# Attention by 32 states and a squared-ReLU MLP on one core: tiny tiles in a pool of their own, another token order for x, clamps of the weight decode on VectorE, program order held on TensorE, a new order of steps

## The chip, the cores and the metric

The kernel runs on one core of a Trainium2 chip. Its engines, as the profile names them, are PE (TensorE, matrix products; PEld is its weight load), DVE (VectorE), ACT (ScalarE), POOL (GpSimd) and SP (SyncE, which here issues nearly all DMAs). Each engine takes its instructions in the order of its own queue, and an instruction waits there for the semaphores of what it needs. The metric is device time in microseconds (us) of one execution; lower is better.

## The reference

```python
# x: 8 batches x 8 heads x 512 tokens x 64, state: 8 x 8 x 32 x 64, w_in: 512 x 2048, w_out: 2048 x 512
scores = scale * x @ state^T;   a  = softmax(scores, last axis);   xread = a  @ state
scores2 = scale * state @ x^T;  a2 = softmax(scores2, last axis);  sread = a2 @ x
y = concatenate([xread, sread], axis=2)          # per batch 512 + 32 rows, heads side by side: 512 columns
h = maximum(y @ w_in, 0);  out = (h * h) @ w_out # 4352 rows
```

The weights come as 64-bit floats, the rest as 32-bit floats, and the output is 32-bit.

## The kernel before, in words

**Products in three parts.** A 32-bit value is split into a high part that TensorE takes in its fast fp32r format and the low rest. Each product is then three matmuls: high by high, high by low, low by high (`mm3`, line 284). `split` (line 265) makes the parts: ACT rounds the high part, DVE or POOL subtracts it.

**The weights are decoded on the chip.** `load_raw` (line 500) and `load_wo` (604) bring 512 KB pieces of the 64-bit weights, 16 of each. `decode` (297) turns one piece into 32-bit floats: ACT takes the absolute value of the high words (line 303), a clamp follows (304, on DVE or on POOL), and three DVE instructions shift and join the bits (305 to 307). `decode_wi` decodes half of a column block of `w_in` (256 columns, `hb` = 0 to 7) and stores it to DRAM for later; `prep_wo` decodes a row block of `w_out` (`fc` = 0 to 15) and splits it into parts that stay in SBUF.

**Attention.** The scores of a batch have only 32 states per head, so state @ w_in is computed once for each pair of batches and column block (`direct_w2`, `later_w2`, `last_w2`; the products are "w2"). The first product of the MLP for tokens is then softmax(scores) times w2, with 256 rows to contract. The batches 0 to 5 keep w2 in DRAM and load it back (`load_w2`), 6 and 7 store it already split. For each batch: `start` and `load` issue the loads of x, `prep` brings x into transposed form (batches 0 and 1 by TensorE, `px`; the others by DVE's 32 by 32 stream transpose, line 364), `scores` multiplies by the states, `transposed_scores`, `softmax` and `exp_s` make the two softmaxes, `transposes` and `sread` the reads for the states. x for batches 2 to 7 comes in 16 DMAs a batch (line 352), each for 32 partitions, in runs of 32 floats.

**The MLP.** `hidden(blk, fc)` (617) makes one block of 128 hidden rows for the 512 tokens of batch `blk`: 6 matmuls into `ph` (two PSUM buffers), ReLU and square on ACT or on ACT and DVE, and the split into `g_hi` (ACT) and `g_lo` (DVE, line 641). `accumulate(blk, fc)` (644) adds its product with `w_out`: 12 matmuls into `acc`. Block 8 holds the 256 rows of the states and has 12 narrower matmuls per hidden step and 6 per accumulate.

**What sets the order.** `PLAN` (line 24) is the program order of all steps, written by hand; `accumulate` runs two to three steps behind `hidden`. The framework then schedules the instructions of each engine by a model of their times, with the program order as priority, so that an engine's queue can differ from `PLAN` unless `keep_in_program_order` ties an instruction behind the one traced before it on its engine. Before the change that is done for the loads of `w_out` and for runs of small matmuls (`in_a_row`, 311). Batches 0 and 1 alternate in groups of four `fc` (0.0 to 0.3, 1.0 to 1.3, 0.4 ...), because the decode of the weights goes on beside them. `SECOND` (183) lists, per kind of operation, the cases that take the second of two engines: for `decode_wi` and `decode_wo` the second is POOL, for `w_out_lo`, `sm_sub`, `sm_mul`, `k_lo`, `w2_lo` it is DVE, for `xT`, `eT`, `out`, `w2_out` it is DVE instead of ACT. The small per-row results of the softmaxes (`m1`, `s1`, `m2`, `nb2`, `s2`, `r2`) lie in the same pool, `p2`, as the large tiles.

Of the kernel before, what the change touches and what calls it, by code (L numbers as in the profile page):

```python
# [19 lines left out]
F64_HI_MIN = 2.0**-15  # L20
# [17 lines left out]
    hidden.0.5 decode_wi.9 load_raw.11 direct_w2.4 prep_wo.8 accumulate.1.3
    hidden.0.6 decode_wi.10 decode_wi.11 load_raw.12 load_wo.10 states.2 accumulate.0.4
    hidden.0.7 load_raw.13 direct_w2.5 load_wo.11 decode_wi.12 accumulate.0.5  # L40
    hidden.1.4 prep_wo.9 load_raw.14 accumulate.0.6
    hidden.1.5 decode_wi.13 load_wo.12 load_raw.15 direct_w2.6 prep_wo.10 load_w2.0.4 load_wo.13
        accumulate.0.7
    hidden.1.6 decode_wi.14 decode_wi.15 direct_w2.7 load_wf.1.0 start.2 load.2.1 prep_wo.11 accumulate.1.4
# [3 lines left out]
    hidden.0.10 later_w2.2.2 later_w2.2.4 load_wf.1.3 prep_wo.14 load_w2.0.7 accumulate.0.8
    hidden.0.11 prep.2.1 prep_wo.15 accumulate.0.9
    hidden.0.12 scores.2 transposed_scores.2.0 exp_s.2.0 transposed_scores.2.1 exp_s.2.1 load_w2.1.4  # L50
        accumulate.0.10
# [155 lines left out]
def tile_attn_moe(  # L207
# [56 lines left out]

    def split(hi, lo, src, key):

        nc.scalar.copy(hi, src)  # L267
        pick(key, nc.gpsimd, nc.vector).tensor_sub(lo, src, hi.bitcast(F32))  # L268
# [42 lines left out]
    def in_a_row(calls):  # L311

        for i, call in enumerate(calls):
            if i == 0:
                call()  # L315
                continue
# [556 lines left out]
```

## Time and profile before

| what | value |
|---|---|
| runs | 740.28, 741.85, 741.93 us; median 741.85 |
| the profiled execution | 738.05 us, span 736.3 us |
| mean granted TensorE clock | 0.988 |
| instructions | 11411 |
| PE, PEld busy | 681.8 and 516.6 us |
| DVE, ACT, POOL busy | 388.5, 335.1 and 130.6 us |
| DMA | 100.36 MB, mean 136 GB/s |

The span runs from the first to the last instruction. A row of a table of windows gives, for a stretch of the span, the busy time of each engine with the number of its instructions, then the granted clock of TensorE (1.00 is full speed), the mean busy share of the 16 DMA engines and what they moved. In a timeline row the columns are start, duration, engine, line, operation, output<-input, shape, count, and in brackets how long the engine had been idle and what it waited for.

### The profile page before, as it was taken

How to read it: one execution, taken by the hardware profiler on the slowest of the kernel's cores; microseconds unless marked ns; L12 is line 12 of the kernel's file. 1: busy time of each engine (PE TensorE's matmuls, PEld its weight loads, DVE VectorE, ACT ScalarE, POOL GpSimd, SP SyncE). 2: the span in 40 equal slices, each digit the busy share in tenths (PEclk: the TensorE clock that was granted, in tenths of full speed). 3: DMA queues.
4: the chain of work that ended last, by engine and by line, in shares of the span. 5: the costliest groups of instructions: out<-in, count | busy, mean ns of one | idle time of the engine just before them, and what ended most of it. 6: DMA issues, size and time to landing. Idle time of an engine off the chain costs nothing.

```text
span 736.3 us, 11411 instructions
## 1 busy us (share of the span) xinstructions
PE 681.8 (93%) x4365; PEld 516.6 (70%) x4365; DVE 388.5 (53%) x665; ACT 335.1 (46%) x643; POOL 130.6 (18%) x92
## 2 busy tenths in 40 slices
...
GB/s 233 280 155 147 100 231 220 190 260 302 59 237 213 188 256 195 72 72 145 163 42 109 146 170 75 69 148 139 58 86 144 60 83 78 94 57 58 29 1 85
DMA packets 120711, 100.36 MB, mean 136 GB/s; under 512 B 68049, under 2 KB 96977, under 8 KB 120657
## 3 DMA queue, kind: packets, MB, share of 16 engines
...
q14 instruction: 21, 0.16, 0.1%
q10 hardware_dynamic: 144, 0.13, 0.1%
...
## 4 chain that ended last, share of the span: by engine, by line
PE 74%; DVE 7%; issue 6%; DMA 5%; SPq 3%; ACT 2%; POOL 2%; DVEq 0%; ACTq 0%; POOLq 0%
PE acc L290 45%; PE ph L290 23%; PE w2ps L318 2%; DMA wi_raw<-in_moe_w_in_dram 2%; SPq L352 1%; DMA wo_raw<-in_moe_w_out_dram 1%; PE w2ps L315 1%; POOL dec L304 1%; DVE dec L307 1%; PE pr L318 1%; DVE wf L306 1%; DMA std<-in_state_dram 1%; DVE dec L306 1%; PE st L315 1%; DMA xp<-in_x_dram 1%
## 5 line engine op out<-in xcount | busy, mean ns | idle before, releaser
L290 PE MATMUL acc<-wo,g_hi 128*128 128x512 f32 x1086 | 322.5, 400 | 0.3 <-ACT g_hi L636 0.3
L290 PEld LDWEIGHTS acc<-wo,g_hi 128*128 128x128 f32 x1086 | 204.0, 189 | 54.8 <-issue 3.5
L290 PE MATMUL ph<-k_hi,w 128*128 128x512 f32 x512 | 185.6, 404 | 6.4 <-DVE g_lo L641 3.9
L290 PE MATMUL acc<-wo,g_lo 128*128 128x512 f32 x543 | 191.4, 397 | 0.0
L641 DVE TENSOR_TENSOR g_lo<-ph,g_hi 128x512 fp32r<-128x512 f32 (+1 forms) x140 | 92.1, 658 | 145.2 <-ACT g_hi L636 141.1
L290 PEld LDWEIGHTS ph<-k_hi,w 128*128 128x128 f32 x512 | 97.3, 191 | 41.5 <-DVE g_lo L641 9.5
L290 PEld LDWEIGHTS acc<-wo,g_lo 128*128 128x128 f32 x543 | 101.0, 189 | 24.9 <-issue 2.1
L636 ACT CAST g_hi<-ph 128x512 fp32r<-128x512 f32 (+1 forms) x144 | 81.1, 564 | 63.3 <-DVE ph L635 57.8
L290 PE MATMUL ph<-k_lo,w 128*128 128x512 f32 x256 | 102.2, 399 | 0.0
L635 DVE SCALAR_TENSOR_TENSOR ph<-ph,r 128x512 f32<-128x512 f32 (+1 forms) x76 | 50.1, 659 | 93.3 <-ACT r L634 93.3
L634 ACT ACTIVATE r<-ph 128x512 f32<-128x512 f32 (+1 forms) x76 | 43.3, 570 | 108.4 <-PE ph L290 108.3
L630 ACT ACTIVATE ph<-ph 128x512 f32<-128x512 f32 (+1 forms) x68 | 38.8, 570 | 76.7 <-PE ph L290 76.7
L268 POOL TENSOR_TENSOR w<-w_f,w 128x512 fp32r<-128x512 f32 x19 | 24.8, 1304 | 216.2 <-ACT w L267 190.0
L290 PEld LDWEIGHTS ph<-k_lo,w 128*128 128x128 f32 x256 | 48.7, 190 | 12.2 <-issue 1.6
L631 ACT ACTIVATE ph<-ph 128x512 f32<-128x512 f32 (+1 forms) x68 | 38.8, 570 | 1.4
L318 PE MATMUL w2ps<-wf,sT 64*32 64x256 f32 x960 | 37.7, 407 | 0.9 <-ACT w L554 0.5
L268 POOL TENSOR_TENSOR s<-sf,s 128x512 fp32r<-128x512 f32 x8 | 10.4, 1299 | 138.2 <-ACT s L267 138.2
L315 PE MATMUL w2ps<-wf,sT 64*32 64x256 f32 x64 | 21.0, 409 | 13.9 <-DVE r L409 7.8
L304 POOL TENSOR_SCALAR wf<-wf 128x512 f32<-128x512 f32 x13 | 26.3, 2027 | 39.1 <-ACT wf L303 35.6
L304 POOL TENSOR_SCALAR dec<-dec 128x512 f32<-128x512 f32 x13 | 26.8, 2070 | 30.9 <-ACT dec L303 30.9
L364 DVE STREAM_TRANSPOSE xT<-xp 128x512 f32<-128x512 f32 x24 | 25.0, 1089 | 13.7 <-DMA xp<-in_x_dram 11.5
L267 ACT CAST w<-w_f 128x512 fp32r<-128x512 f32 x40 | 24.6, 614 | 3.8 <-DMA w_f<-w_d 3.7
...
## 6 DMA issues: line engine op xcount, KB each, us to landing
...
```

The costliest lines, as they stand in the source:

```text
L268: pick(key, nc.gpsimd, nc.vector).tensor_sub(lo, src, hi.bitcast(F32))
L290: m = nc.tensor.matmul(ps, l, r, start=first and i == 0, stop=last and i == len(seq) - 1, skip_group_check=skip)
L304: eng.tensor_scalar(vf, vf, F64_HI_MIN, F64_HI_MAX, ALU.max, ALU.min)
L315: call()
L318: tc.keep_in_program_order(call())
L364: nc.vector.transpose(xT[:, c].rearrange("p (k s j) -> p k j s", k=KC, j=4), self.xp[g][:, c].rearrange("p (j k d) -> p k j d", j=4, k=KC),)
L630: nc.scalar.activation(ph, ph, AF.Relu)
L631: nc.scalar.activation(ph, ph, AF.Square)
L634: nc.scalar.activation(r, ph, AF.Relu)
L635: nc.vector.scalar_tensor_tensor(ph, ph, 0.0, r, ALU.max, ALU.mult)
L636: nc.scalar.copy(ghi, ph)
L641: nc.vector.tensor_sub(glo, ph, ghi.bitcast(F32))
```

## The change

Six edits:

1. The six tiny tiles go from pool `p2` to a new pool `p3` of the same depth.
2. The DMAs of x for batches 2 to 7 write the tokens in the order (k, j) instead of (j, k) along a partition, so that the stream transpose reads and writes 512 elements in one run each; before, both sides were strided.
3. Of 26 clamps on POOL, 24 go to DVE: all 13 of `decode_wo` and 11 of 13 of `decode_wi` (6 and 10 stay).
4. `behind` ties ten chosen DVE instructions to the DVE instruction traced before them: the clamps of `decode_wi` 2, 7, 15 and `decode_wo` 0, 1, 2, 12, and the first reduction of `exp_s` 0.0, 0.1, 2.1.
5. From step `hidden.2.8` on, every TensorE instruction is held in program order.
6. `PLAN` is rewritten up to `hidden.2.4`, and a few entries of `SECOND` change engine (`k_lo.1.0`, `w2_lo.1.5`, `w_out_lo.10`, `xT.1.1.1` to DVE; `k_lo.2.1` to POOL; `w2_out.2.2.1` to ACT; `hidden.1.12` squares on DVE instead of ACT).

```diff
-    load_raw.0 load_states.0 ident neg_ident load_raw.1 start.0 load.0.1 decode_wi.0 load_wo.1 decode_wi.1
-        states.0 prep.0.0 prep.0.1 load_raw.2 scores.0 start.1 load.1.1 direct_w2.0 transposed_scores.0.0
-        exp_s.0.0 softmax.0.0 load_raw.3 load_wo.0 transposed_scores.0.1 exp_s.0.1 softmax.0.1 decode_wi.2
-        decode_wi.3 prep_wo.0 direct_w2.1 prep.1.0 load_wo.2 prep.1.1
-    hidden.0.0 prep_wo.1 load_wo.3 transposes.0
-    hidden.0.1 scores.1 transposed_scores.1.0 exp_s.1.0 transposed_scores.1.1 exp_s.1.1 prep_wo.2 load_raw.4
-    hidden.0.2 load_raw.5 softmax.1.0 softmax.1.1 load_wo.4 sread.0 accumulate.0.0
-    hidden.0.3 decode_wi.4 decode_wi.5 load_wo.5 load_raw.6 load_raw.7 accumulate.0.1
-    hidden.1.0 direct_w2.2 transposes.1 prep_wo.4 load_wo.6 load_wo.7 accumulate.0.2
-    hidden.1.1 decode_wi.6 decode_wi.7 prep_wo.3 sread.1 load_raw.8 load_raw.9 accumulate.0.3
+    load_raw.0 ident neg_ident start.0 load.0.1 load_states.0 load_raw.1 states.0 decode_wi.0 prep.0.0
+        load_raw.2 load_wo.0 decode_wi.1 direct_w2.0 prep_wo.0 load_wo.1 decode_wi.2 start.1 load.1.1
+    prep_wo.1 load_raw.3 decode_wi.3 prep.0.1 scores.0 transposed_scores.0.1 softmax.0.1 exp_s.0.1
+        transposed_scores.0.0 softmax.0.0 exp_s.0.0 hidden.0.0 load_wo.2 load_wo.3
+    hidden.0.1 prep_wo.2 prep.1.0 prep.1.1 scores.1 transposed_scores.1.0 load_raw.5 transposed_scores.1.1
+        load_raw.4
+    prep_wo.3 softmax.1.0 softmax.1.1 load_wo.4 accumulate.0.0
+    exp_s.1.0 exp_s.1.1 direct_w2.1 hidden.0.2 hidden.0.3 transposes.0 sread.0 load_wo.5 accumulate.0.1
+    hidden.1.0 decode_wi.4 load_raw.6 decode_wi.5 load_raw.7 direct_w2.2 load_wo.6 load_wo.7 accumulate.0.2
+    hidden.1.1 transposes.1 prep_wo.4 decode_wi.6 load_raw.8 decode_wi.7 direct_w2.3 load_raw.9
+        accumulate.0.3
...
-    hidden.1.12 load_part.1 accumulate.1.10
-    hidden.1.13 load_w2.2.0 later_w2.6.2 later_w2.6.4 load_wf.1.7 accumulate.1.11
-    hidden.1.14 start.3 accumulate.1.12
-    hidden.1.15 load_wf.2.0 load_w2.2.1 later_w2.7.2 load.3.1 later_w2.7.4 accumulate.1.13
+    hidden.1.12 start.3 load_part.1 accumulate.1.10
+    hidden.1.13 load_wf.1.7 accumulate.1.11 load_w2.2.0
+    hidden.1.14 accumulate.1.12
+    hidden.1.15 load_w2.2.1 later_w2.7.2 later_w2.7.4 load_wf.2.0 accumulate.1.13
     hidden.2.0 accumulate.1.14
     hidden.2.1 load_w2.2.2 accumulate.1.15
-    hidden.2.2 prep.3.0 accumulate.2.0
-    hidden.2.3 load_w2.2.3 accumulate.2.1
-    hidden.2.4 last_w2.0 load_wf.2.1 accumulate.2.2
+    hidden.2.2 load.3.1 prep.3.0 accumulate.2.0
+    hidden.2.3 later_w2.6.2 load_w2.2.3 accumulate.2.1
+    hidden.2.4 later_w2.6.4 last_w2.0 load_wf.2.1 accumulate.2.2
     hidden.2.5 prep.3.1 load_w2.2.4 accumulate.2.3
...
+PINNED_FROM = "hidden.2.8"
...
-    decode_wi: 1 4 5 6 7 8 9 10 11 12 13 14 15
-    decode_wo: 0 1 2 3 4 6 7 8 9 11 13 14 15
+    decode_wi: 6 10
...
+    pin: decode_wi.2 decode_wi.7 decode_wi.15 decode_wo.0 decode_wo.1 decode_wo.2 decode_wo.12 exp_s.0.0
+        exp_s.0.1 exp_s.2.1
...
+    p3 = ctx.enter_context(tc.tile_pool(name="p3", bufs=2))
...
+    def behind(key, op):
+
+        if f"pin.{key}" in second:
+            tc.keep_in_program_order(op)
...
-        nc.tensor.matmul(ps, neg["ident"], hi, start=False, stop=True, skip_group_check=True)
+        in_order(nc.tensor.matmul(ps, neg["ident"], hi, start=False, stop=True, skip_group_check=True))
+
+    pinned = []
+
+    def in_order(m):
+
+        if pinned:
+            tc.keep_in_program_order(m)
+        return m
...
-            if pin:
+            if pin or pinned:
                 tc.keep_in_program_order(m)
...
-        eng.tensor_scalar(vf, vf, F64_HI_MIN, F64_HI_MAX, ALU.max, ALU.min)
-        nc.vector.tensor_scalar(v, v, 3, 0x3FFFFFFF, ALU.logical_shift_left, ALU.bitwise_and)
+        clamp = eng.tensor_scalar(vf, vf, F64_HI_MIN, F64_HI_MAX, ALU.max, ALU.min)
+        if eng is nc.vector:
+            behind(key, clamp)
+        shift = nc.vector.tensor_scalar(v, v, 3, 0x3FFFFFFF, ALU.logical_shift_left, ALU.bitwise_and)
+        if eng is nc.gpsimd:
+            behind(key, shift)
...
             if i == 0:
-                call()
+                in_order(call())
                 continue
...
+                        x_v = x[b, 4 * g + 2 * c + h].rearrange("(j s k) d -> s k j d", j=4, k=KC)
                         nc.sync.dma_start(
-                            xp[o : o + 32, c].rearrange("p (t d) -> p t d", d=32),
-                            x[b, 4 * g + 2 * c + h].rearrange("(s t) d -> s t d", s=32)[..., 32 * e : 32 * e + 32],
+                            xp[o : o + 32, c].rearrange("p (k j d) -> p k j d", k=KC, d=32),
+                            x_v[..., 32 * e : 32 * e + 32],
                         )
...
-                    nc.vector.transpose(
-                        xT[:, c].rearrange("p (k s j) -> p k j s", k=KC, j=4),
-                        self.xp[g][:, c].rearrange("p (j k d) -> p k j d", j=4, k=KC),
-                    )
+                    nc.vector.transpose(xT[:, c], self.xp[g][:, c])
...
-            nc.vector.transpose(sp, self.st[g])
+            behind(f"transposed_scores.{b}.{g}", nc.vector.transpose(sp, self.st[g]))
...
-            m2 = p2.tile([P, 1], F32, tag="m2", name=f"m2{b}_{g}")
-            nc.vector.tensor_reduce(m2, st, AX.X, ALU.max)
+            m2 = p3.tile([P, 1], F32, tag="m2", name=f"m2{b}_{g}")
+            behind(f"exp_s.{b}.{g}", nc.vector.tensor_reduce(m2, st, AX.X, ALU.max))
...
-                    nc.tensor.transpose(pt[:, ts(k, P)], e2[:, k], ident)
+                    in_order(nc.tensor.transpose(pt[:, ts(k, P)], e2[:, k], ident))
...
+        if k == PINNED_FROM:
+            pinned.append(k)
```

More of the change, by code (lines that the diff above doesn't have):

```diff
@@ L31 @@
-    hidden.0.2 load_raw.5 softmax.1.0 softmax.1.1 load_wo.4 sread.0 accumulate.0.0
-    hidden.0.3 decode_wi.4 decode_wi.5 load_wo.5 load_raw.6 load_raw.7 accumulate.0.1
-    hidden.1.0 direct_w2.2 transposes.1 prep_wo.4 load_wo.6 load_wo.7 accumulate.0.2
-    hidden.1.1 decode_wi.6 decode_wi.7 prep_wo.3 sread.1 load_raw.8 load_raw.9 accumulate.0.3
-    hidden.1.2 direct_w2.3 prep_wo.5 prep_wo.6 accumulate.1.0
-    hidden.1.3 prep_wo.7 load_wo.8 load_wo.9 accumulate.1.1
-    hidden.0.4 load_states.2 decode_wi.8 load_raw.10 accumulate.1.2
@@ L38 @@
[L38 to L44, printed above, removed]
@@ L45 @@
-    hidden.1.7 load_w2.0.5 later_w2.0.2 later_w2.0.4 load_wf.1.1 prep_wo.12 load_wo.14 accumulate.1.5
-    hidden.0.8 load_wo.15 later_w2.1.2 later_w2.1.4 load_wf.1.2 prep_wo.13 load_w2.0.6 accumulate.1.6
+    load_raw.0 ident neg_ident start.0 load.0.1 load_states.0 load_raw.1 states.0 decode_wi.0 prep.0.0
+        load_raw.2 load_wo.0 decode_wi.1 direct_w2.0 prep_wo.0 load_wo.1 decode_wi.2 start.1 load.1.1
+    prep_wo.1 load_raw.3 decode_wi.3 prep.0.1 scores.0 transposed_scores.0.1 softmax.0.1 exp_s.0.1
+        transposed_scores.0.0 softmax.0.0 exp_s.0.0 hidden.0.0 load_wo.2 load_wo.3
@@ new lines @@
+    hidden.1.2 prep_wo.5 sread.1 accumulate.1.0
+    hidden.1.3 prep_wo.6 prep_wo.7 load_wo.8 load_wo.9 accumulate.1.1
+    hidden.0.4 load_states.2 decode_wi.8 accumulate.1.2
+    hidden.0.5 decode_wi.9 load_raw.11 direct_w2.4 prep_wo.8 accumulate.1.3 load_wo.10 load_raw.10
+    hidden.0.6 decode_wi.10 load_raw.12 states.2 accumulate.0.4
+    hidden.0.7 decode_wi.11 load_raw.13 load_wo.11 accumulate.0.5
+    hidden.1.4 prep_wo.9 decode_wi.12 load_raw.14 accumulate.0.6
+    hidden.1.5 decode_wi.13 load_raw.15 direct_w2.6 prep_wo.10 direct_w2.5 load_w2.0.4 load_wo.12
+        accumulate.0.7 load_wo.13
@@ L47 @@
+    hidden.1.6 decode_wi.14 decode_wi.15 direct_w2.7 load_wf.1.0 start.2 load.2.1 later_w2.0.2 prep_wo.11
+        accumulate.1.4
+    hidden.1.7 prep_wo.13 load_w2.0.5 load_wf.1.1 later_w2.0.4 prep_wo.12 load_wo.14 accumulate.1.5
+    hidden.0.8 load_wo.15 later_w2.1.2 load_wf.1.2 load_w2.0.6 accumulate.1.6
     hidden.0.9 prep.2.0 accumulate.1.7
[L48 to L51, printed above, removed]
+    hidden.0.10 later_w2.2.2 later_w2.2.4 load_wf.1.3 prep_wo.14 accumulate.0.8
@@ L52 @@
+    hidden.0.11 prep.2.1 prep_wo.15 load_w2.0.7 accumulate.0.9
+    hidden.0.12 scores.2 transposed_scores.2.0 exp_s.2.0 transposed_scores.2.1 exp_s.2.1 later_w2.1.4
+        load_w2.1.4 accumulate.0.10
     hidden.0.13 softmax.2.0 load_n.2.0 load_part.0 accumulate.0.11
-    hidden.0.14 later_w2.3.2 later_w2.3.4 load_wf.1.4 later_w2.4.2 load_w2.1.5 accumulate.0.12
+    hidden.0.14 later_w2.3.2 later_w2.3.4 load_wf.1.4 later_w2.4.2 load_w2.1.5 later_w2.4.4 accumulate.0.12
     hidden.0.15 softmax.2.1 load_n.2.1 accumulate.0.13
@@ L55 @@
     hidden.1.8 transposes.2 accumulate.0.14
-    hidden.1.9 later_w2.4.4 load_wf.1.5 load_w2.1.6 accumulate.0.15
+    hidden.1.9 load_wf.1.5 load_w2.1.6 accumulate.0.15
     hidden.1.10 sread.2 accumulate.1.8
     hidden.1.11 later_w2.5.2 later_w2.5.4 load_wf.1.6 load_w2.1.7 accumulate.1.9
-    hidden.1.12 load_part.1 accumulate.1.10
-    hidden.1.13 load_w2.2.0 later_w2.6.2 later_w2.6.4 load_wf.1.7 accumulate.1.11
-    hidden.1.14 start.3 accumulate.1.12
-    hidden.1.15 load_wf.2.0 load_w2.2.1 later_w2.7.2 load.3.1 later_w2.7.4 accumulate.1.13
+    hidden.1.12 start.3 load_part.1 accumulate.1.10
```

25 lines of the change are left out of this document (12 added, 13 removed).

## The prediction

> **What bounds the kernel now.** I read the page's busy shares first, then the table of windows, then the timeline of the engines where PE stands still.
>
> ```profile
> PE 681.8 (93%) x4365; PEld 516.6 (70%) x4365; DVE 388.5 (53%) x665; ACT 335.1 (46%) x643; POOL 130.6 (18%) x92
> ```
>
> ```profile
> 0.00:17.50 17.50, 6.51 (x48) 3.05 (x48) 5.91 (x11) 3.94 (x7) 2.62 (x7) 1.00 0.95 232
> 17.50:45.00 27.50, 10.07 (x68) 5.12 (x69) 27.39 (x49) 13.16 (x30) 19.33 (x12) 1.00 0.68 197
> 45.00:83.00 38.00, 30.22 (x238) 20.57 (x240) 37.69 (x70) 25.63 (x53) 23.65 (x14) 0.91 0.57 182
> 83.00:120.00 37.00, 30.97 (x264) 21.05 (x257) 26.19 (x43) 20.98 (x43) 17.51 (x10) 0.92 0.62 207
> 120.00:160.00 40.00, 39.84 (x273) 29.10 (x272) 28.57 (x41) 20.12 (x38) 11.21 (x7) 0.99 0.65 190
> 160.00:200.00 40.00, 37.20 (x273) 25.89 (x273) 22.84 (x44) 18.31 (x37) 8.33 (x7) 1.00 0.64 211
> 200.00:260.00 60.00, 55.54 (x526) 37.74 (x525) 27.41 (x42) 22.70 (x42) 1.42 (x2) 0.97 0.70 199
> 260.00:720.00 460.00, 460.00 (x2644) 364.86 (x2643) 207.77 (x363) 205.39 (x392) 46.56 (x37) 1.00 0.35 102
> 720.00:736.30 16.30, 11.45 (x53) 9.18 (x51) 4.69 (x8) 4.88 (x10) 0.00 (x0) 0.97 0.33 97
> ```
>
> The columns after the stretch are PE, PEld, DVE, ACT, POOL, granted clock, DMA share, GB/s. PE is the bound, but not everywhere: from 260 to 720 it is busy 460.00 of 460.00 us, so an order change can win nothing there and only lose. Its idle time, stretch less busy, is 10.99, 17.43, 7.78, 6.03, 0.16, 2.80, 4.46, 0 and 4.85 us: 54.5 in all, of which 49.7 lie before 260. From 17.5 to 83 DVE is busy 65.1 of 65.5 us: there DVE is the bound, and PE waits for decoded weights and softmaxes. Nearly all that can be won sits in those stretches and in how early they begin. The profiled execution took 738.05 us (span 736.3 and 1.75 around it); the median of the runs is 3.8 us above it, and I carry that over.
>
> **Clamps from POOL to DVE.** A clamp on each engine, then the three DVE instructions that follow it:
>
> ```profile
> L304 POOL TENSOR_SCALAR wf<-wf x13: 1915/1922/2368, 8.8 to 121.1; 128x512 f32<-128x512 f32 x13
> L304 DVE TENSOR_SCALAR wf<-wf x3: 426/427/782, 5.5 to 24.5; 128x512 f32<-128x512 f32 x3
> L305 DVE TENSOR_SCALAR wf<-wf x16: 384/428/1527, 6.6 to 123.4; 128x512 uint32<-128x512 uint32 x16
> L306 DVE SCALAR_TENSOR_TENSOR wf<-wi_raw,wf x16: 676/692/1682, 7.0 to 124.9; 128x512 uint32<-128x512 uint32 x16
> L307 DVE SCALAR_TENSOR_TENSOR wf<-wi_raw,wf x16: 643/690/1420, 7.7 to 126.7; 128x512 uint32<-128x512 uint32 x16
> ```
>
> ```profile
> L306 DVE SCALAR_TENSOR_TENSOR wf<-wi_raw,wf 128x512 uint32<-128x512 uint32 x16 | 13.9, 872 | 0.3
> L307 DVE SCALAR_TENSOR_TENSOR dec<-wo_raw,dec 128x512 uint32<-128x512 uint32 x16 | 13.5, 842 | 0.2
> L307 DVE SCALAR_TENSOR_TENSOR wf<-wi_raw,wf 128x512 uint32<-128x512 uint32 x16 | 13.1, 817 | 0.2
> L305 DVE TENSOR_SCALAR wf<-wf 128x512 uint32<-128x512 uint32 x16 | 12.2, 761 | 4.2 <-POOL wf L304 3.4 <-DMA wo_raw<-in_moe_w_out_dram 0.8
> L306 DVE SCALAR_TENSOR_TENSOR dec<-wo_raw,dec 128x512 uint32<-128x512 uint32 x16 | 12.2, 761 | 0.2
> L305 DVE TENSOR_SCALAR dec<-dec 128x512 uint32<-128x512 uint32 x16 | 8.6, 535 | 5.1 <-POOL dec L304 5.1
> L268 DVE TENSOR_TENSOR k_lo<-aT,k_hi 128x512 fp32r<-128x512 f32 x9 | 8.4, 936 | 2.5 <-ACT k_hi L267 2.5
> L268 DVE TENSOR_TENSOR wo<-dec,wo 128x512 fp32r<-128x512 f32 x8 | 5.4, 680 | 0.3 <-ACT wo L267 0.3
> ```
>
> Minimum, median and maximum stand in the first fence, count, busy and mean in the second. Instructions of one shape have a median of 0.43 or 0.69 us and a maximum of 1.4 to 1.7: they are held up while POOL works. The means of the decode lie above the medians by 0.180, 0.152, 0.127, 0.333, 0.069 and 0.107 us; the sum, 0.968, times 16 is 15.5 us of DVE time lost, and 9 subtractions for `k_lo` lose 0.256 each against those for `wo`, 2.3 more. Against that, 24 clamps at 0.427 add 10.2 us. The last column says that DVE also stood idle 8.5 us behind POOL clamps.
>
> What of this reaches PE goes by stretch. Of the 26 POOL clamps 15 run between 17.5 and 83, the first and the last of these being:
>
> ```profile
> 26.21 3.93 POOL L304 TENSOR_SCALAR dec<-dec 128x512 f32<-128x512 f32 x2
> 78.39 4.31 POOL L304 TENSOR_SCALAR dec<-dec 128x512 f32<-128x512 f32 x2
> ```
>
> So 15.5 x 15/26 = 8.9, and with the 2.3 some 11 us, are lost there. POOL is busy 43.0 us in it, about 31 of that with clamps: if the loss falls to them by that share 8 us go, if wholly 11. On DVE 15 clamps cost 15 x 0.427 = 6.4, or 4.9 if they overlap their neighbours by 0.1 each, an estimate. Net 1.6 to 6.1; DVE is the bound there, so PE gets it one to one. I take 4.5. From 83 to 120 DVE has slack (26.19 of 37), and a shorter decode helps only where PE waits for it: 0 to 3, I take 1.5.
>
> The Trainium skill's page "GPSIMD Engine Reference", section 4.1, says that one-input elementwise work on GpSimd runs at roughly line rate. By that a POOL clamp would cost about what DVE's does and the move would only load DVE: some 10 us the other way in this term. The rows disagree, 1.92 against 0.427 us, so it gets no chance of its own.
>
> At 160 us one clamp is on the path by itself:
>
> ```profile
> 158.03 1.92 POOL L304 TENSOR_SCALAR dec<-dec 128x512 f32<-128x512 f32 x1 [15.70 <-ACT dec L303]
> 159.98 1.49 DVE L305 TENSOR_SCALAR dec<-dec 128x512 uint32<-128x512 uint32 x1 [4.08 <-POOL dec L304]
> 162.12 0.50 PE L290 MATMUL ph<-k_hi,w 128*128 128x512 f32 x1 [2.12 <-DVE g_lo L641]
> ```
>
> DVE's queue stands 4.08 us behind a POOL clamp, `g_lo` is queued behind that, PE waits 2.12. On DVE the clamp costs 0.43: 1.7 us gained, 0 to 2.1.
>
> **The new start.** The loads of x for batch 0 are issued first:
>
> ```profile
> 1.24 1.93 SPq L483 DMA_DIRECT2D std<-in_state_dram  x4
> 3.70 5.79 SPq L438 DMA_DIRECT2D xn<-in_x_dram  x8
> 8.73 3.93 PE L373 MATMUL px<-ident,xn 128*128 128x128 f32 x14 [8.73 <-DMA xn<-in_x_dram]
> 45.01 0.78 PE L290 MATMUL ph<-k_lo,w 128*128 128x512 f32 x1
> ```
>
> PE starts on x at 8.73 and has its first steady run of `hidden` at 45.01. Moving eight issues ahead of `std` and a weight load brings them from 3.70 to about 1.2, 2.5 us earlier; the four loads of the states (1.93 us of SP) and the second weight load pay 5.8 us on SP's queue, and the states are needed only with `w2` and the scores. Before `hidden.0.0` the program now leaves out `prep.1`, `direct_w2.1` and their splits, but adds `prep_wo.1`, one decode, and puts `decode_wi.2`, `decode_wi.3` ahead of the scores. Upper bound: DVE is idle 11.6 us in the first window (17.50 - 5.91), and if the order fills that, everything starts that much earlier. Lower bound, below nothing: the three decodes that now come ahead of the softmaxes cost 3 x (0.43 + 0.43 + 0.69 + 0.69) = 6.7 us of DVE that PE then waits for, less the 2.5: -4. I take +5, since part of the idle DVE time waits for loads that come earlier now, and DMA is already at 0.95.
>
> **Clock.** PE's first matmuls after a gap run at half pace:
>
> ```profile
> 46.43 0.63 PE L290 MATMUL ph<-k_lo,w 128*128 128x512 f32 x1
> 46.86 0.63 PE L290 MATMUL ph<-k_hi,w 128*128 128x512 f32 x1
> 569.99 2.33 PE acc L290 x10
> ```
>
> 0.43 us from start to start here, 0.233 later. Besides, busy time at a lower granted clock costs 30.22 x 0.09 + 30.97 x 0.08 + 55.54 x 0.03 = 6.9 us. Fewer gaps return some: 0 to 7, I take 2.5. The Trainium skill's page "TensorE: Matmul & The Clock Gate", Part 1, has half the clock after an idle window of about 3.4 us until as long a busy one: by it each long gap that goes would return up to 1.7 us, an estimate; the pace at 46 us agrees.
>
> **Batch 3's loads.**
>
> ```profile
> L352 SPq DMA_DIRECT2D xp<-in_x_dram x96: 566/625/1664, 137.7 to 460.3; - x96
> DMA to landing us min/median/max: 2.2/2.8/5.9
> 239.16 1.08 DVE L364 STREAM_TRANSPOSE xT<-xp 128x512 f32<-128x512 f32 x1 [3.53 <-DMA xp<-in_x_dram]
> 242.00 0.62 PE L315 MATMUL w2ps<-wf,sT 64*32 64x256 f32 x2 [3.15 <-ACT w2o L278]
> ```
>
> DVE's queue stands behind a transpose whose x has not landed, the splits behind it, and PE waits 3.15 of the 4.46 us of this window. A step is 18 matmuls x 0.233 = 4.2 us. `start.3` moves from two steps ahead of `hidden.2.0` to four, on SP's queue past the four reads of `load_part.1`, two weight reads and the stores of `later_w2.6`; `load.3.1` goes to three steps before `prep.3.1`: 12.6 us for 8 x 0.625 + 2.8 to 5.9 = 7.8 to 10.9. That covers it by 1.7. In return `later_w2.6` comes near `last_w2.0`. I take 3; bounds -2 to 4.5.
>
> **The rest.** The transposes without strides: 20 of 24 lie after 220, most under a full PE, so nothing. The runs of 32 floats and their number stay, so the loads cost the same; a fourth dimension could lengthen the 0.625 us issue, within the bounds above. The tiny pool moves addresses only, on which no row here depends; I take 0, and 1 us either way as an estimate. Held PE order: nothing to gain at 460.00 of 460.00. In program order `hidden` i needs the `ph` buffer of i-2; between lie 2.8 + 1.4 + 2.8 = 7.0 us of matmuls, against four instructions of ACT and DVE in a row, at 0.69 (the row of L306, same shape) 2.8. `transposes.7` stands directly ahead of `sread.7`, whose input is a copy of some 0.7 us: about 1 us. I take -1; 0 to -18 (below).
>
> **Sum.** 4.5 + 1.5 (clamps) + 1.7 (the one at 160) + 5 (start) + 2.5 (clock) + 3 (batch 3) - 1 (held order) = 17.2. 738.05 - 17.2 = 720.85, and 3.8 more: 725 us.
>
> **Rivals.** *Loads bound the start.* DMA is at 0.95 in the first window; if weights land no sooner, the start gives 0, the clamps half and the clock 1: 3 + 1.7 + 1 + 3 - 1 = 7.7, so 734. The same would come of it if the framework's model left the queues of the start much as they were, the program order being only a priority there. Against it: a share of 0.68 and 0.57 right after.
>
> *Tied clamps block DVE: slower.* Seven clamps are tied behind the DVE instruction traced before them. Such a clamp waits for ACT's absolute value, that for a load, and all softmax and split work is queued behind it, PE behind that.
>
> ```profile
> ACT dec L303 <- DMA wo_raw<-in_moe_w_out_dram: 13.8, 9, 3.4
> ```
>
> Total, times, longest. At 3.4 us each, 7 cost 24: 749. It decides from 17.2/7 = 2.5 us a clamp. Against it: before, the mean wait is 13.8/9 = 1.5, and a tie only keeps a clamp from coming earlier.
>
> *Held PE order stalls.* With DVE or ACT over 4.2 us late (7.0 - 2.8), PE can no longer take other matmuls meanwhile. Six batches with three such places (`scores`, `transposes`, `sread`), about 1 us each as for `transposes.7`, are 18 us: 743. For it: nothing on PE may pass a wait any more. Against it: DVE is busy 207.77 of 460.
>
> **Numbers.** Forecast 0.60, loads 0.17, held order 0.10, tied clamps 0.13. About 0.3%, 2.2 us, is what a measurement can tell from no change. Forecast and loads are faster (0.77), held order about the same (0.10), tied clamps slower (0.13). The forecast's own range: from half its sum, 8.6, so 733, to the terms at their high ends (6.1 + 3 + 2.1 + 11.6 + 7 + 4.5 = 34.3), 708, which will hardly all come together: 709. The whole range goes from there over the loads' 734 to the held order's 743, and leaves out the tied clamps and a little below 709.
>
> **What would show it.** Right: DVE's L305 to L307 near their medians in every row, no wait of DVE on POOL L304 but for two; the steady run of `hidden` starts at 36 to 42; PE idle before 260 near 35 us (49.7 less the 17.2 without the clock's 2.5); still 0 idle after. Wrong: idle PE after 260, a DVE wait on ACT L303 of several us with PE behind it, or the steady run after 45.

## The result, and the profile after

| | before | after |
|---|---|---|
| median of the runs, us | 741.89 (740.28 to 742.72, 4 runs) | 706.58 (705.40 to 707.57, 4 runs) |
| ratio, 95% interval | | 0.9526 (0.9504 to 0.9548) |
| profiled execution, us | 738.05, span 736.3 | 706.18, span 704.4 |

The kernel became 4.7% faster, some 35 us, and 18 us faster than forecast: 706.6 lies below the forecast's 725 and below its range. The busy shares and the same stretches as before; the columns are PE, PEld, DVE, ACT, POOL, granted clock, DMA share, GB/s:

```profile
PE 660.6 (94%) x4365; PEld 512.0 (73%) x4365; DVE 375.3 (53%) x691; ACT 334.7 (48%) x643; POOL 78.2 (11%) x66
```

```profile
0.00:17.50 17.50, 7.65 (x56) 3.10 (x63) 8.19 (x15) 4.84 (x7) 0.98 (x7) 1.00 0.96 231
17.50:45.00 27.50, 17.61 (x91) 11.72 (x76) 25.81 (x56) 15.41 (x32) 7.24 (x6) 0.91 0.71 195
45.00:83.00 38.00, 30.28 (x257) 20.23 (x257) 36.78 (x77) 26.21 (x58) 5.68 (x4) 0.93 0.50 163
83.00:120.00 37.00, 34.49 (x290) 25.98 (x289) 31.76 (x59) 24.29 (x47) 5.97 (x3) 1.00 0.70 229
120.00:160.00 40.00, 34.73 (x306) 23.76 (x304) 24.86 (x42) 19.95 (x36) 4.51 (x4) 1.00 0.94 288
160.00:200.00 40.00, 38.98 (x383) 27.79 (x376) 23.91 (x46) 21.12 (x41) 8.25 (x7) 1.00 0.61 196
200.00:260.00 60.00, 58.39 (x451) 42.53 (x450) 25.43 (x41) 23.31 (x42) 1.29 (x1) 1.00 0.81 229
260.00:690.00 430.00, 428.96 (x2523) 349.01 (x2516) 195.19 (x353) 195.18 (x375) 44.24 (x36) 1.00 0.33 97
690.00:704.40 14.40, 9.56 (x46) 7.84 (x44) 3.37 (x7) 4.40 (x8) 0.00 (x0) 0.92 0.38 109
```

PE's idle time before 260 fell from 49.7 to 37.9 us (stretch less busy, summed), close to the 35 forecast, but not in the places forecast: the start comes earlier than expected, and there is new idle time, 5.27 of 40 us from 120 to 160, where the DMA share is now 0.94. That the sum agrees is in part luck. But the span fell by 31.9 us and the idle time only from 54.5 to 43.7, so 21 us came out of PE's *busy* time, with the same 4365 matmuls. Two views show how. First the chain that ended last, before and then after, at the same time in the run:

```profile
568.61 1.39 PE ph L290 x6
```

```profile
568.73 2.72 PE acc L309 x12
571.45 1.36 PE ph L309 x6
```

The prediction's row from 569.99 has 2.33 us for 10 matmuls of `acc`; now 12 take 2.72, so 227 ns from start to start instead of 233. In the trace the mean time from start to start of neighbouring 512-column matmuls of `hidden` and `accumulate` (2401 recorded in all, here those from 260 to 400 us) went from 232.6 to 227.3 ns. Second, the windows of the tiles `acc` and `ph` alone (PE busy, then clock, DMA share, GB/s), the two rows of before first:

```profile
0.00:260.00 260.00, 101.04 (x384) 0.97 0.67 200
0.00:260.00 260.00, 62.08 (x218) 0.97 0.67 200
```

```profile
0.00:260.00 260.00, 116.10 (x444) 0.98 0.74 220
0.00:260.00 260.00, 67.09 (x244) 0.98 0.74 220
```

602 of these matmuls before 260 us became 688: 86 more, 20 us at 0.233. Of that, 11.8 us is idle time that went, and 5.2 us comes from the small products `w2ps`, whose windows hold 774 matmuls in 37.78 us before and 806 in 32.63 after; the other 3 us are the remaining small products and the overlap of neighbouring matmuls. Over the whole span `w2ps` keeps PE busy for 40.29 us instead of 48.97, with the same 1030 matmuls. These 8.7 us and 2401 matmuls at 5.3 ns less each, 12.7 us, make an estimate of 21.4 for the 21 us of busy time.

The decode, in the table of lines (busy and mean, then the idle time before and what ended it), and the start on PE:

```profile
L329 DVE SCALAR_TENSOR_TENSOR wf<-wi_raw,wf 128x512 uint32<-128x512 uint32 x16 | 11.8, 745 | 0.2
L326 DVE TENSOR_SCALAR wf<-wf 128x512 uint32<-128x512 uint32 x16 | 8.5, 537 | 0.8 <-POOL wf L323 0.6
L326 DVE TENSOR_SCALAR dec<-dec 128x512 uint32<-128x512 uint32 x16 | 6.7, 419 | 0.1
L323 DVE TENSOR_SCALAR dec<-dec 128x512 f32<-128x512 f32 x16 | 7.4, 463 | 6.0 <-ACT dec L322 6.0
```

```profile
5.59 4.78 PE L394 MATMUL px<-ident,xn 128*128 128x128 f32 x16 [5.59 <-DMA xn<-in_x_dram]
28.11 0.78 PE L309 MATMUL ph<-k_lo,w 128*128 128x512 f32 x1
```

The means of 872, 761 and 535 ns are now 745, 537 and 419, and DVE waits 0.6 us for POOL where it waited 8.5. The last row has a new wait, 6.0 us for ACT's absolute values, 4.78 of them in one piece before the clamp at 129.49 us. PE starts on x 3.1 us earlier, and the first matmul of `hidden` comes at 26.4 instead of 38.6. The longer run of `hidden`, at 45.0 before, begins at 28.1, earlier than the 36 to 42 forecast, though gaps follow it (PE is busy 17.61 of the 27.5 us up to 45). The pace and this start are what the forecast did not have.

### The profile page after: what moved, and what is told of

Read it like the earlier page. It is cut to its first block, busy times and chain, and to the rows that moved or that the text cites. A ratio compares the mean times of both kernels' runs of the same rounds, so it can differ in the third digit from the quotient of the medians.

```text
span 704.4 us, 11391 instructions
## 1 busy us (share of the span) xinstructions
PE 660.6 (94%) x4365; PEld 512.0 (73%) x4365; DVE 375.3 (53%) x691; ACT 334.7 (48%) x643; POOL 78.2 (11%) x66
## 4 chain that ended last, share of the span: by engine, by line
PE 71%; DVE 9%; DMA 9%; SPq 4%; ACT 3%; issue 2%; POOL 0%; DVEq 0%; ACTq 0%
PE acc L309 43%; PE ph L309 22%; DMA wi_raw<-in_moe_w_in_dram 3%; SPq L376 2%; DMA w_d<-w2o 2%; DMA wo_raw<-in_moe_w_out_dram 2%; PE w2ps L341 1%; PE w2ps L338 1%; PE pt L472 1%; DVE wf L329 1%; DMA xp<-in_x_dram 1%; PE st L338 1%; DMA win_f<-wf 1%; DMA wf<-win_f 1%; DVE wf L330 1%
## 5 line engine op out<-in xcount | busy, mean ns | idle before, releaser
L309 PE MATMUL acc<-wo,g_hi 128*128 128x512 f32 x1086 | 338.6, 397 | 8.0 <-ACT wo L278 3.0
L309 PE MATMUL acc<-wo,g_lo 128*128 128x512 f32 x543 | 208.0, 392 | 0.0
L309 PE MATMUL ph<-k_hi,w 128*128 128x512 f32 x512 | 180.8, 395 | 5.8 <-DVE g_lo L662 2.7
L657 ACT CAST g_hi<-ph 128x512 fp32r<-128x512 f32 (+1 forms) x144 | 81.2, 565 | 49.7 <-DVE ph L656 42.4
L309 PE MATMUL ph<-k_lo,w 128*128 128x512 f32 x256 | 100.6, 393 | 0.1
L655 ACT ACTIVATE r<-ph 128x512 f32<-128x512 f32 (+1 forms) x77 | 43.7, 568 | 107.3 <-PE ph L309 107.0
L651 ACT ACTIVATE ph<-ph 128x512 f32<-128x512 f32 (+1 forms) x67 | 38.0, 567 | 98.1 <-PE ph L309 98.1
L652 ACT ACTIVATE ph<-ph 128x512 f32<-128x512 f32 (+1 forms) x67 | 38.1, 569 | 1.4
L341 PE MATMUL w2ps<-wf,sT 64*32 64x256 f32 x960 | 35.8, 390 | 0.7 <-ACT srd L494 0.7
L388 DVE STREAM_TRANSPOSE xT<-xp 128x512 f32<-128x512 f32 x24 | 16.0, 693 | 18.7 <-PE st L341 9.5
L338 PE MATMUL w2ps<-wf,sT 64*32 64x256 f32 x64 | 20.1, 395 | 5.9 <-DVE wf L330 4.0
L309 PE MATMUL ph<-sr_hi,s 128*128 128x256 f32 x128 | 25.5, 282 | 0.0
L309 PEld LDWEIGHTS ph<-sr_hi,s 128*128 128x128 f32 x128 | 21.0, 191 | 0.6
```

The lines of the kernel that those rows point to most:

```text
L309: m = nc.tensor.matmul(ps, l, r, start=first and i == 0, stop=last and i == len(seq) - 1, skip_group_check=skip)
L338: in_order(call())
L341: tc.keep_in_program_order(call())
L388: nc.vector.transpose(xT[:, c], self.xp[g][:, c])
L651: nc.scalar.activation(ph, ph, AF.Relu)
L652: nc.scalar.activation(ph, ph, AF.Square)
```

## The experiments

My theory after the two traces was that the pace comes from the addresses: in the built program g_hi and g_lo, the stationary tiles of `accumulate`, start 192 bytes beyond a multiple of 512 in the kernel before (the tiny tiles lie ahead of them) and 128 beyond in the changed one. Its rival was the held PE order. For the early gain, order of steps, clamps and holds on DVE were taken apart.

The columns count, in each trace, when the n-th recorded matmul of `hidden` and `accumulate` starts (us from the span's start); the last is the time from the 650th to the 2330th, where little but the pace is at work. Each comes from one execution; the two traces of the changed kernel differ by up to 0.9 us in these columns. Ratios are to the kernel before on the same chip.

| run | kernel | median us | ratio (95%) | 1st | 300th | 650th | 650 to 2330 |
|---|---|---|---|---|---|---|---|
| | before | 737.7 to 741.9 | | 38.6 | 156.3 | 273.5 | 438.9 |
| | after | 706.58 | 0.9526 (0.9504 to 0.9548) | 26.4 | 139.7 | 249.0 | 433.4 |
| e5 | after, again | 707.47 | 0.9559 (0.9513 to 0.9606) | 25.8 | 139.9 | 249.9 | 433.4 |
| e1 | after, tiny tiles in p2 | 713.60 | 0.9681 (0.9638 to 0.9724) | 25.7 | 137.6 | 248.8 | 441.1 |
| e3 | after, g 64 bytes on | 713.21 | 0.9670 (0.9630 to 0.9710) | 26.0 | 138.0 | 247.0 | 441.1 |
| e12 | after, g 32 bytes on | 715.43, one run | | 26.3 | 139.8 | 251.6 | 439.7 |
| e2 | before, wide tiny tiles | 729.53 | 0.9887 (0.9846 to 0.9929) | 39.3 | 154.8 | 271.6 | 431.0 |
| e4 | after, PE not held | 705.22 | 0.9557 (0.9508 to 0.9605) | 26.3 | 139.9 | 248.4 | 432.2 |
| e7 | before, new order | 723.60 | 0.9782 (0.9731 to 0.9833) | 29.9 | 135.6 | 255.3 | 440.5 |
| e9 | before, new order to accumulate.0.1 | 735.72 | 0.9950 (0.9918 to 0.9982) | 30.5 | 140.3 | 269.7 | 439.2 |
| e15 | before, new order to accumulate.1.5 | 730.95 | 0.9908 (0.9873 to 0.9942) | 30.0 | 135.6 | 265.3 | 438.8 |
| e10 | before, new order from there on | 736.41 | 0.9977 (0.9942 to 1.0011) | 38.6 | 154.3 | 269.9 | 440.6 |
| e8 | before, clamps on DVE | 741.83 | 1.0028 (1.0002 to 1.0054) | 34.5 | 155.3 | 273.3 | 440.1 |
| e6 | after, clamps on POOL | 711.85 | 0.9621 (0.9581 to 0.9661) | 26.9 | 137.6 | 254.4 | 433.4 |
| e11 | after, old tokens, no DVE holds | 717.52 | 0.9702 (0.9647 to 0.9758) | 33.9 | 139.6 | 257.2 | 437.9 |
| e14 | after, no DVE holds | 715.86 | 0.9700 (0.9670 to 0.9731) | 33.9 | 141.4 | 258.8 | 433.4 |
| e17 | after, only exp_s held | 713.21 | 0.9648 (0.9599 to 0.9697) | 30.3 | 137.9 | 255.7 | 433.4 |
| e18 | after, only clamps held | 714.30 | 0.9681 (0.9622 to 0.9740) | 28.6 | 137.1 | 254.6 | 433.4 |
| e13 | after, old tokens | 709.15 | 0.9615 (0.9576 to 0.9653) | 25.6 | 138.1 | 245.4 | 437.9 |
| e16 | after, old tokens, PE not held | 706.60 | 0.9592 (0.9545 to 0.9640) | 25.7 | 137.5 | 245.6 | 432.4 |

### Addresses: e1, e2, e3, e12

The edits, one for each run, with every engine's instructions in the same order as in the kernel that they start from:

```
e1   all six p3.tile(...) -> p2.tile(...)
e2   m2 = p2.tile([P, 1], ...)     -> p2.tile([P, 32], ...)[:, :1]      (before; nb2, s2, r2 alike)
     m1 = p2.tile([P, J], ...)     -> p2.tile([P, 32], ...)[:, :J]      (before; s1 alike)
e3   aT = p2.tile([P, S], ...)     -> p2.tile([P, S + 16], ...)[:, :S]  (tag aT; eT gets 112 more, so that, counted from a
     multiple of 512 bytes, only g and eT move)
e12  the same with 8 and 120
```

> The changed kernel with its tiny tiles back in the pool p2, every engine's instructions in the same order; only addresses move (g_hi and g_lo from 128 to 192 beyond a multiple of 512 bytes). Address theory: the 512-column matmuls of the steady state go back from 226-227 ns a start to 231-236, and with some 2400 of them 12 to 20 us come back: 719 to 727 us. Order theory (the held PE order gives the pace): nothing moves, 705 to 708 us with 226-227 ns.

> The kernel before with every tiny tile widened to 128 bytes in the same pool, every engine's instructions in the same order, so that all large tiles start at a multiple of 128 bytes. Address theory, if a multiple of 128 bytes is what counts: 512-column matmuls at 226-227 ns instead of 231-236 and 12 to 20 us less than before, 722 to 730 us, with the start of the kernel before. Address theory with a multiple of 512 (or the distance between two tiles) as what counts: still 742 us. Order theory: 740 to 743 us.

> The changed kernel with only g_hi, g_lo and eT 64 bytes further on, all else at its address and in its order. Address theory, if it is the stationary tiles g that matter: the same as with the tiny tiles back, 719 to 727 us, 231-236 ns a matmul. If other tiles matter (the staging tiles of decode, the scratch of Relu, the output tiles): 705 to 708 us. Order theory: 705 to 708 us.

> The changed kernel with g_hi, g_lo and eT 32 bytes further on (160 beyond a multiple of 512), all else in its place and order. If any start off a multiple of 128 bytes costs the same: 232 to 233 ns a 512-column matmul and 712 to 715 us. If the price grows with the pieces of 32 bytes: 235 ns or more and 718 us or more. If only 64 matters: 227 ns and 705 to 708 us.

Rows of the chain from e1, e2 and e12:

```profile
558.88 2.80 PE acc L309 x12
```

```profile
571.37 2.27 PE acc L290 x10
```

```profile
556.31 2.79 PE acc L309 x12
```

In e1 12 matmuls take 2.80 us again, in e2 10 take 2.27. From the 650th to the 2330th matmul e1 needs 7.7 us more than e5, e2 7.9 less than before. By the ratios e2 gains 8.3 us (0.0113 of 738), and e1 and e3 lose 8 to 11 against the two runs of the changed kernel. e3 moves only g_hi, g_lo and eT and loses the same as e1, so it is these; eT has no part in `hidden` and `accumulate`, which leaves g. e2 has g at 384 beyond a multiple of 512 and is as fast as with 128; at 160 (e12, one run) and 192 the pace is slow alike, 231.5 and 232.5 ns. The address theory stands, with less than its 12 to 20 us: the pace moves by some 5.2 ns, but the first 650 matmuls mostly wait for other work, and 1751 x 5.2 ns is 9.1 us. The order theory falls with e1 and with e4.

### The held PE order: e4

```
-        if k == PINNED_FROM:
-            pinned.append(k)
```

> The changed kernel without the held PE order (PINNED_FROM never comes). Address theory: the pace stays at 226-227 ns and the time within 2 us, 705 to 709 us. Order theory: 512-column matmuls return to 231-236 ns and 12 to 20 us come back, 719 to 727 us. The forecast's own term for the held order was a cost of 1 us, with an end at 18 us: by it 689 to 706 us.

The pace stays at 227 ns, and 0.9557 against 0.9526 and 0.9559 is no difference. The hold does not make the pace. Between the 650th and the 2330th matmul it costs 1.2 us in the traces (433.4 against 432.2), which the times cannot tell from none.

### The order of steps: e7, e9, e15, e10

```
e7   before.py with the PLAN of the changed kernel
e9   its steps up to accumulate.0.1, then what is left in the old order
e15  its steps up to accumulate.1.5, then what is left in the old order
e10  the old steps up to accumulate.1.5, then what is left in the new order
```

> The kernel before with the new order of steps alone: clamps, tokens, pools and engines as before. The forecast's terms for the order were 5 us at the start and 3 us for the loads of batch 3: 731 us against 739 us. If the order carries the whole gain of the first 280 us: 715 us. If the order needs the clamps on DVE: 737 us or more, since the decode of the first tiles moves earlier behind 1.9 us clamps on POOL.

> The kernel before with the new order of steps up to accumulate.0.1 and the old order for all that is left. The order alone took 739.2 to 723.6 us. The forecast gave the start 5 us: 734 us. If the start carries all that the order gives: 722 to 725 us. If the old order behind it gives the lead back, as the clamps' lead of 8 us at the 160th matmul of hidden and accumulate was given back by the 300th: 737 us or more.

> The kernel before with the new order of steps up to accumulate.1.5 and the old order behind it. The whole new order took off 15.6 us, its first five lines 2.3 to 3.7, its part from hidden.0.8 on 1.6. If the middle lines keep the lead of the start: 725 us. If the parts simply add with nothing in the middle: 734 us.

> The kernel before with the old order of steps up to accumulate.1.5 and the new order for the rest, in which the loads of batch 3 move ahead. The forecast gave these loads 3 us: 736 us. If they carry a good part of what the order gives: 732 us or less. If nothing: 738 to 741 us.

The order alone gives 15.6 us, twice the forecast's 8. PE's busy time on `w2ps`, 48.97 us before and 40.29 after, is 44.40 in e7 and 48.64 in e2: about half of that drop comes with the order and hardly any with the addresses. Why the same matmuls take less was not settled. The order's gain is no sum of its parts: the new start by itself is 16 us ahead at the 300th matmul (140.3 against 156.3) and 3.8 ahead at the 650th. In e9, between 140 and 172 us, the table of waits has (total, times, longest):

```profile
ACT w2o L197 <- DMA part_d<-po: 7.0, 1, 7.0
DVE po L623 <- DMA w_d<-w2o: 4.4, 1, 4.4
ACT dec L222 <- DMA wo_raw<-in_moe_w_out_dram: 4.0, 1, 4.0
PE ph L209 <- ACT w L186: 3.6, 1, 3.6
```

ACT and DVE, now early, run into stores and loads that are not yet through: their output tiles wait for stores to drain. PE idles 7.3 us in this stretch where it idled 2.8 before. The rest of the lost lead was not followed to single waits. The middle lines keep more of the lead (8.2 us at the 650th in e15), the whole order 18.2. The late part alone, with batch 3's loads, gives 1.6 us with an interval that holds none.

### The clamps: e8, e6

```
e8   SECOND of before: decode_wi: 1 4 5 6 ... 15 -> 6 10;  decode_wo: (none)
e6   SECOND of after: both lists back as before
```

> The kernel before with its decode clamps on DVE (as the change chooses them), all else as before. The forecast's terms: 7.7 us, 731 us against 739 us. If they carry the whole gain of the first 280 us: 715 us. If they gain only with the new order of steps: 736 to 740 us. The rival in which DVE is delayed by the clamps: 745 us or more.

> The changed kernel with the clamps of decode on POOL wherever the kernel before had them, all else (order of steps, tokens, addresses) as changed. The forecast's terms for the clamps were 4.5, 1.5 and 1.7 us: by them 714 us. If the clamps carry the whole gain of the first 280 us (24 us in the traces): 728 us. If the order of steps carries it: 705 to 709 us.

Alone the clamps gain nothing (1.0028); beside the rest they are worth 4.4 us (711.85 against 707.47 in the same series). e8 is 8 us ahead at the 160th matmul (109.1 against 117.2 us) and 1.0 at the 300th. Between the two, its views show the loads of the tile `wi_raw` (from 105 to 125 us), then the timelines of ACT, DVE and PE:

```profile
L503 SPq DMA_DIRECT2D wi_raw<-in_moe_w_in_dram x2: 385/404/424, 111.1 to 112.5; - x2
...
DMA to landing us min/median/max: 5.3/6.6/7.9
```

```profile
116.46 0.66 ACT L302 ACTIVATE wf<-wi_raw 128x512 f32<-128x512 f32 x1 [3.31 <-issue]
...
120.47 0.66 ACT L302 ACTIVATE wf<-wi_raw 128x512 f32<-128x512 f32 x1 [1.63 <-DMA wi_raw<-in_moe_w_in_dram]
```

```profile
117.15 0.43 DVE L303 TENSOR_SCALAR wf<-wf 128x512 f32<-128x512 f32 x1 [5.92 <-ACT wf L302]
```

```profile
120.15 0.50 PE L289 MATMUL ph<-k_hi,w 128*128 128x512 f32 x1 [0.93 <-DVE g_lo L640]
127.26 0.50 PE L289 MATMUL ph<-k_hi,w 128*128 128x512 f32 x1 [1.64 <-DVE g_lo L640]
135.31 0.71 PE L289 MATMUL acc<-wo,g_hi 128*128 128x512 f32 x2 [2.23 <-ACT wo L266]
```

The loads issued at 111.1 and 112.5 land at 111.1 + 5.3 = 116.4 and 112.5 + 7.9 = 120.4, just as ACT goes on (the first wait has no releaser in the trace, so its cause is read from these times). The clamp waits for ACT's absolute value, that for the load, and DVE's whole queue stands 5.92 us behind the clamp; PE waits for `g_lo` and `wo` after it, 4.8 us in the three rows, of the 7 that the lead shrinks by. In the kernel before the same wait stood on POOL, where nothing that PE needs at once was queued (waits from 95 to 145 us):

```profile
POOL wf L304 <- ACT wf L303: 12.4, 3, 8.1
```

The move took a slow clamp from POOL and put a wait for a load on DVE. It pays once the order brings the loads earlier.

### The holds on DVE: e11, e14, e17, e18

```
e11  old loads of xp and strided transposes, and no pin: line
e14  no pin: line
e17  pin: exp_s.0.0 exp_s.0.1 exp_s.2.1
e18  pin: decode_wi.2 decode_wi.7 decode_wi.15 decode_wo.0 decode_wo.1 decode_wo.2 decode_wo.12
```

> The changed kernel with x loaded in the old order of tokens, the transposes with strides, and without the ten holds on DVE. The forecast gave both nothing: 705 to 709 us. If the transposes (24, 0.4 us longer each with strides) were on the path of PE: up to 9 us more, 716 us. If the holds keep DVE in the order that the new start needs: 710 us or more.

> The changed kernel without the ten holds on DVE, all else as changed. If the holds carry the 10 us: 715 to 718 us, with the first hidden at 34 us instead of 26. If the transposes do: 705 to 709 us, the late start being made up before the 200th matmul as in the run with both.

> The changed kernel with the holds on the three exp_s maxima alone; the seven decode clamps are free. If it is the maxima of the second softmax that ran ahead of the first (in the run without holds aT stood on DVE at 29.1 and 30.6 us instead of 21.2 and 24.4): aT at 21 to 25 us and 705 to 709 us. If the free clamps push the softmax back: 714 to 717 us.

> The changed kernel with the holds on the seven decode clamps alone; the maxima of exp_s are free. If the clamps were what pushed the softmax back: aT at 21 to 25 us and 705 to 709 us. If the maxima were: 714 to 717 us. If tied clamps block DVE, as the forecast's slower rival has it, this run is the slowest of all: 716 us or more, with DVE idle several us behind ACT's absolute values. If both are needed, neither this nor its counterpart comes under 710.

The holds carry the loss of e11: without them 715.9 us, which is 8 more than e5 by the medians and 10 by the ratios. DVE's queue without them (e14), then with them (e5):

```profile
15.58 0.65 DVE L414 TENSOR_REDUCE m<-st 128x1 f32<-128x512 f32 x1
...
18.31 0.65 DVE L414 TENSOR_REDUCE m<-st 128x1 f32<-128x512 f32 x1
...
29.08 0.69 DVE L447 STREAM_TRANSPOSE aT<-sp 128x512 f32<-128x512 f32 x1
...
30.61 0.70 DVE L447 STREAM_TRANSPOSE aT<-sp 128x512 f32<-128x512 f32 x1
```

```profile
21.16 0.70 DVE L449 STREAM_TRANSPOSE aT<-sp 128x512 f32<-128x512 f32 x1
...
24.42 0.70 DVE L449 STREAM_TRANSPOSE aT<-sp 128x512 f32<-128x512 f32 x1
25.04 0.65 DVE L416 TENSOR_REDUCE m<-st 128x1 f32<-128x512 f32 x1
```

aT is what the first `hidden` waits for. Without holds the maxima for the other softmax (m from st, needed much later) and the clamps and decodes go first, and aT comes at 30.6. With the maxima held alone (e17) a clamp and its decode still go ahead, and the second aT stands at 28.00; with the clamps held alone (e18) the maxima do, and it stands at 27.20:

```profile
18.21 0.41 DVE L322 TENSOR_SCALAR dec<-dec 128x512 f32<-128x512 f32 x1
...
28.00 0.71 DVE L448 STREAM_TRANSPOSE aT<-sp 128x512 f32<-128x512 f32 x1
```

```profile
15.39 0.65 DVE L415 TENSOR_REDUCE m<-st 128x1 f32<-128x512 f32 x1
...
27.20 0.69 DVE L448 STREAM_TRANSPOSE aT<-sp 128x512 f32<-128x512 f32 x1
```

The first `hidden` follows the second aT by 1.4 to 3.3 us in all four. Both kinds are needed: neither run comes under 710. No tied clamp blocked DVE: in the changed kernel DVE idles at most 0.2 us before any of the seven.

### The tokens: e13, e16

```
e13  old loads of xp and strided transposes
e16  the same, and PINNED_FROM never comes
```

> The changed kernel with the old order of tokens and the transposes with strides alone; the holds on DVE stay. With both taken back the time was 717.5 us, some 10 more than the changed kernel. If the transposes carry that: 715 to 718 us, lost after the 200th matmul of hidden and accumulate. If the holds on DVE carry it: 705 to 709 us.

> The changed kernel with the old order of tokens and strided transposes and without the held PE order. If the longer transposes cost time only where PE may not take other matmuls meanwhile: about 4 us of the 10 come back, those lost behind 260 us, 711 us. If they cost it everywhere: the same as with the held order, 715 to 718 us.

```profile
260.00:690.00 430.00, 425.82 (x2498) 345.18 (x2497) 196.42 (x347) 193.94 (x373) 42.93 (x35) 1.00 0.32 97
```

```profile
260.00:690.00 430.00, 430.00 (x2516) 348.96 (x2515) 199.15 (x351) 196.17 (x376) 43.72 (x35) 1.00 0.32 97
```

With strided transposes and the held order (e13) PE idles 4.2 us behind 260; without the hold (e16) it does not. But with the old tokens the 650th matmul also comes 2.8 to 4.5 us earlier (e16 against e4, e13 against e5). In sum the span of e13 is that of e5, 705.3 us, and the ratios 0.9615 and 0.9559 have overlapping intervals. So the new tokens gain behind 260 us only under the held order, and in neither pair is a difference of the sums measurable (without the hold 0.9592 against 0.9557). Why they cost time early was not settled. No run beat the changed kernel clearly; e4 and e16 equal it.

## Why the prediction was wrong, point by point

- **"PE is busy 460.00 of 460.00 us, so an order change can win nothing there", and "the tiny pool moves addresses only, on which no row here depends; I take 0".** These are the steps that failed. PE was busy, but at 232.6 ns where 227.3 is possible, and the addresses set that. Measured: 8 to 11 us (e1, e2, e3) instead of 0, with 1 either way. Full occupancy is no proof of full pace, and the trace of before already hinted at it:

```profile
559.32 1.37 PE ph L290 x6
```

  These six go at 228 ns. From 260 to 680 us 94 of 419 starts within `hidden` follow the one before after 224 to 228 ns, but only 6 of 1004 within `accumulate`, whose stationary tiles are g_hi and g_lo. The Trainium skill's page "Perfetto Trace Analysis", section "Identifying the Most-Contended Engine", says that the busy share of matmuls is no good measure of the headroom that is left. The traces agree: the span fell by 31.9 us and PE's busy time by 21.2 with the same matmuls.
- **The 3.8 us between profile and median, carried over.** After the change the profiled execution lies 0.4 us under the median, so 3.4 of the miss is this.
- **The new start, +5, of the order's 8.** Mis-sized: the order alone gives 15.6 (e7), and the start keeps its lead only with the rest of the order (e9: 2 to 4). I costed a start by the instructions moved ahead of `hidden.0.0`, and not by the loads and stores that the lead then runs into.
- **Clamps, 4.5 + 1.5 + 1.7.** The mechanism was right row by row (means near the medians, no waits on POOL), the size was 4.4 in its place (e6) and nothing alone (e8). The term took DVE as the only bound of the stretch.
- **Tied clamps block DVE, the slower rival.** Its mechanism is real, but it showed with *free* clamps in the old order (e8: 5.92 us behind one clamp). The changed kernel has one such wait too, the forecast's own sign of being wrong: 4.78 us at 129.49, behind the clamp of `decode_wo` 13, which is free as well, and PE then waits 1.17 us for `g_lo` at 136.58. The ties themselves did the opposite: with the held maxima they are worth 8 to 10 us (e14), which the forecast gave nothing.
- **Loads bound the start.** Not the start, but the lead behind it: a DMA share of 0.94 from 120 to 160, and the waits of e9.
- **Clock, +2.5.** By the forecast's way of counting (busy time times the missing share of the clock) the loss fell by 3.2 us, from 6.9 to 3.7 (17.61 x 0.09 + 30.28 x 0.07). But no run shows such a loss as time. Of the 53 runs of the kernel before that stand beside the experiments, 12 had a mean granted clock of 0.959 to 0.965 and 41 one of 0.976 to 0.987; they took 738.8 and 738.9 us in the mean, where 0.02 of some 680 busy us would be 14. So the term is not shown to be worth anything, and the likeness of 2.5 and 3.2 proves nothing.
- **Batch 3's loads, +3.** 1.6 with none in its interval (e10).
- **Held PE order, -1, and the rival at 743.** The size is right in the traces, 1.2 us, and too small to see in the times (e4); the rival's 18 us did not come, PE idles 1.04 of 430 us after 260.
- **Transposes at 0.** In the sum right (e13), as two effects that cancel.

The terms against the runs: 15.6 for the order, 8 to 10 for the holds, 4.4 for the clamps and 8 to 11 for the addresses are 36 to 41, against a measured 32 to 35. The last three were taken out of the whole one by one, so some of them overlap.
